# A linear-attention and SiLU feed-forward kernel: the tensor engine's tiles placed at multiples of 128 bytes

## The chip, the cores and the metric

The kernel runs on one core of one Trainium2 chip. The metric is the time of one execution in microseconds on the device, the median over several runs. TensorE does the matrix products; DVE (VectorE), ACT (ScalarE) and POOL (GpSimd) work on tiles elementwise; SP (SyncE) issues the DMAs. SBUF is the on-chip memory that holds 128 partitions; a tile occupies the same range of bytes in every partition. PSUM is the memory into which TensorE accumulates.

## The reference

```python
def _attn_ref(q, k, v, g_norm):          # q, k, v: 8 batches, 8 heads, 576 tokens, 64 wide
    kv = np.einsum('bhsd,bhse->bhde', k, v)
    out = np.einsum('bhsd,bhde->bhse', q, kv)
    rms = np.sqrt(np.mean(out * out, axis=-1, keepdims=True) + 1e-06)
    return (out / rms * g_norm).astype(np.float32)

def _moe_ref(x, w_in, w_out):            # x: 4608 x 512, w_in: 512 x 2048, w_out: 2048 x 512
    h = x @ w_in
    g = h * (1.0 / (1.0 + np.exp(-h)))
    return (g @ w_out).astype(np.float32)
```

The attention's output, heads side by side, is the `x` of the feed-forward part. All data is float32.

## The kernel before, in words

**Precision.** TensorE has a fast type for 4-byte operands, `float32r`, that keeps fewer bits than float32. The kernel splits an operand into an upper part in that type and the remainder, also in that type, and makes three products (upper by lower, lower by upper, upper by upper) that accumulate in one PSUM bank. A tile of such an operand therefore has a dimension of two, for the two parts. Products of plain float32 tiles are used where little is to be computed: k by v (L253), q by kv for the first two batches (L286, L341), transposes.

**Stages.** The 4608 tokens are nine tiles of 512. For each tile, the 16 blocks of `w_in` (128 features each) give h, transposed (features in the partitions, tokens along the row); ACT applies SiLU; the result is split into `gh` and `gl` and multiplied by the 16 blocks of `w_out` into four PSUM banks, one for each 128 tokens.

- Tiles 0 and 1 compute h plainly: `products` (L474) streams a slice of x (512 columns) against a 128x128 slice of the block `wi`, four slices by three products, twelve matmuls for a block. x of tile 0 lies in the tiles x0 to x3 (x0 to x2 in the `spare` places, x3 in a `late` place), x of tile 1 in `x_second`.
- Tiles 2 to 8 compute h in pairs of blocks by seven half-size products in place of eight, with sums of weights and sums of x: `pair_step` calls `product` (L634) seven times, each six matmuls of 256 columns, 42 for a pair and eight pairs for a tile. The streamed operands are made by `make_operand` in seven places: four in the memory of `x_second`, seen under another shape as `x_operands`, and three in the `spare` places (operand4 to operand6). The weights are slices of the `wi` blocks and of sums that are loaded back from DRAM.
- `project` (L505) multiplies `gh` and `gl` (as weights, 128x128) by `wo` (streamed, 512 columns): twelve matmuls for a block and tile. In the last tile, the last of the four banks is worked in two halves of 256 columns, the second of them in the bank `at`.
- Attention for later batches is fitted in between: k by v (L253), then q by kv in three products of 288 columns (L288 to L290) with the split tiles `kh` and `kl` as weights and `ql` and `qh` streamed.

**Order.** The order on each engine is written out by hand (`tc.manual_schedule()`): lists of jobs for each step, and a list `ORDER` for the loads on SP's queue. The products of `pair_step` and the projections alternate: 42 matmuls of L634, then 24 of L505, with the attention's products of four batches' pairs let in at two places in a tile.

**Places in SBUF.** Each pool hands out places in the order in which tiles or tags first appear, and a tile takes a multiple of 32 bytes in each partition. The pool `const` comes first: four `kvm` tiles (512 bytes each), `ident` (the tag `kh`, two places of 512), then `warm_up` and `gcol` (4 bytes, 32 taken), `both` (the tag `kl`, two places of 512), `d_eps` (32 taken), `x_place`, the three `spare` places, `gap`, the two `late` places. The pools of weights, k/v/q and gated tiles follow. `x_second` is the beginning of `x_place`, and `x_operands` is the same memory 48 elements (192 bytes) further on; the tile `gap` of 16 elements brings the two to 64 elements in all.

Of the kernel before, what the change touches and what calls it, by code (L numbers as in the profile page):

```python
# [8 lines left out]
F32 = mybir.dt.float32  # L9
F32R = mybir.dt.float32r  # L10
# [20 lines left out]
def linear_attention_rms_silu_ffn(  # L31
# [22 lines left out]
    nc = tc.nc  # L54
    B, NP, P, S = q.shape
# [3 lines left out]
    TN = 512  # L59
# [5 lines left out]
    const = ctx.enter_context(tc.tile_pool(name="const", bufs=1))  # L65
# [13 lines left out]
        nc.gpsimd.memset(t, 0.0)  # L79
    ident = const.tile([P, P], F32, name="ident", tag="kh", bufs=2)  # L80
    make_identity(nc, ident)
    warm_up = const.tile([P, 1], F32, name="warm_up")
    nc.gpsimd.memset(warm_up, 1.0)
    gcol = const.tile([P, 1], F32, name="gcol")
    both = const.tile([P, P], F32, name="both", tag="kl", bufs=2)
    nc.gpsimd.tensor_copy(out=both, in_=ident)
    for i in range(4):
        nc.gpsimd.tensor_copy(
            out=both[32 * i:32 * i + 32, 32 * (i ^ 1):32 * (i ^ 1) + 32], in_=ident[32 * i:32 * i + 32, 32 * i:32 * i + 32]
        )  # L90
    d_eps = const.tile([P, 1], F32, name="d_eps")
    nc.gpsimd.memset(d_eps, float(D) * EPS)

    def load_g():
        for h in range(P // D):
            nc.sync.dma_start(out=gcol[h * D:(h + 1) * D, :], in_=g_norm.rearrange("(d o) -> d o", o=1))
# [6 lines left out]

    SHIFT = 48
    x_place = const.tile([P, NP * 2 * TN + SHIFT], F32R, name="x_place")
    x_second = x_place[:, :NP * 2 * TN].rearrange("p (c a n) -> p c a n", c=NP, a=2)
    x_operands = x_place[:, SHIFT:].rearrange("p (c a k n) -> p c a k n", c=NP, a=2, k=2)  # L110
    x_first, lates = {}, {}

    def spare(n, shape, dtype, name):
        return const.tile(shape, dtype, name=name, tag=f"spare{n}")

    def late(n, shape, dtype, name):
        if not lates:
            const.tile([P, 64 - SHIFT], F32, name="gap")
        if name not in lates:
            lates[name] = const.tile(shape, dtype, name=name, tag=f"late{n}")  # L120
        return lates[name]

    def x32(c, w):

        return late(c // 2, [P, 2, TN], F32, f"x32_{c // 2}")[:, c % 2, w]
# [14 lines left out]
    def full_tile(kind, f):  # L140
        if kind == "wo":
            t = late(1, [P, 2, NP * P], F32, "wo_full")[:, f % 2]
        else:
            t = tmp.tile([P, S], F32, name="full", tag="tmp")[:, :NP * P]
        fulls[kind, f] = t
        return t
# [54 lines left out]
    def x_part(t, a, c):  # L201

        if t == 1:
            return x_second[:, c, a]
        if c not in x_first:
            kind = {"shape": [P, 2, TN], "dtype": F32R, "name": f"x{c}"}
            x_first[c] = spare(c, **kind) if c < 3 else late(0, **kind)
        return x_first[c][:, a]
# [386 lines left out]
    def operand(j):  # L595

        if j < 4:
            return x_operands[:, j]
        if j not in operands:
            operands[j] = spare(j - 4, [P, 2, 2, H], F32R, f"operand{j}")  # L600
        return operands[j]
# [20 lines left out]
    def make_operand(m):  # L622
        j, x, _ = seven[m]
        upper, lower = operand(j)[:, 0], operand(j)[:, 1]
        nc.scalar.copy(out=upper, in_=x())
        nc.vector.tensor_tensor(out=lower, in0=x(), in1=upper.bitcast(F32), op=ALU.subtract)

    def product(m, i, out):
        j, _, a_of = seven[m]
        x = operand(j)  # L630
        n = 0
        for c in range(2):
            for a, b in ((0, 1), (1, 0), (0, 0)):
                nc.tensor.matmul(  # L634
                    out=out, lhsT=a_of(i, a, c), rhs=x[:, b, c], start=(n == 0), stop=(n == 5)
                )
                n += 1
# [165 lines left out]
    with tc.manual_schedule():  # L803
# [4 lines left out]
        for item in ORDER.split():  # L808
            kind, n = item.rstrip("0123456789"), int(item.lstrip("wiopbg") or 0)
# [236 lines left out]
```

## Time and profile before

| | |
|---|---|
| median of 3 runs | 839.21 us (839.19 to 839.67) |
| profiled execution | 839.63 us, of which the span of the profile is 837.8 us |
| TensorE matmuls | 5454, busy 826.8 us, 99% of the span |
| TensorE weight loads | 5454, busy 734.6 us (88%), beside the matmuls |
| DVE, ACT, POOL | busy 63%, 43%, 17% |
| granted clock of TensorE | full throughout |
| DMA | 122.55 MB, on the mean 146 GB/s |

A matmul of the profile is two rows: PEld is its weight load, PE the streaming of the other operand through the array. Several are in flight, so the duration of one (389 ns for 512 columns on the page) is not the distance to the next one. That distance, the step, is read where a run of n matmuls stands as one piece: in the chain (each line: start in us, duration in us, what) or from starts in the timeline.

### The profile page before, as it was taken

To read this page: it belongs to the slowest core of one execution; us is meant where nothing else is said; L and a number is where in the kernel's file an instruction comes from. 1 tells how busy PE (TensorE), PEld (TensorE's weight loads), DVE (VectorE), ACT (ScalarE), POOL (GpSimd) and SP (SyncE) were. 2 spreads that over 40 slices of the span, in tenths; PEclk is the share of its full clock that TensorE was granted. 3 is DMA by queue.
4 is the path that set the end of the run, shared out by engine and by line. 5 is a ranking of instruction groups with operands and counts; after the bars stand their busy time and mean duration, and the time that the engine had idled before them with its cause. 6 is when DMAs were issued, how large, how long until landed. Compare 5 with 4: busy or idle time off the path is not lost.

```text
span 837.8 us, 14032 instructions
## 1 busy us (share of the span) xinstructions
PE 826.8 (99%) x5454; PEld 734.6 (88%) x5454; DVE 528.9 (63%) x1027; ACT 359.0 (43%) x744; POOL 145.9 (17%) x142
## 2 busy tenths in 40 slices
PE   8999999999999999999999999999999999999998
PEld 7767888888899999998999998999999999999997
DVE  4886875788476567657766667656865664464332
ACT  3766564534453245325532355225532432243222
POOL 2786983423010002000200011001100000000000
PEclk9999999999999999999999999999999999999999
DMA  8879011337343634364424452444423343334331
GB/s 322 313 257 362 4 57 51 136 145 261 122 161 100 215 115 146 101 214 144 165 91 160 163 173 88 158 158 157 151 84 103 106 155 103 105 102 151 100 102 51
DMA packets 42418, 122.55 MB, mean 146 GB/s; under 512 B 4848, under 2 KB 5104, under 8 KB 42352
## 3 DMA queue, kind: packets, MB, share of 16 engines
q1 hardware_dynamic: 42352, 121.65, 42.4%
q8 instruction: 43, 0.70, 0.4%
q14 instruction: 23, 0.19, 0.1%
HBM read 103.81 MB, written 17.83 MB: 145 GB/s over the span
## 4 chain that ended last, share of the span: by engine, by line
PE 94%; DMA 4%; POOL 1%; ACT 0%; issue 0%; SPq 0%
PE acc L505 46%; PE hp L634 33%; PE hp L474 9%; PE at L253 2%; DMA k<-in_k 1%; DMA wo<-in_moe_w_out 1%; DMA early_wi<-in_v 1%; DMA v<-in_v 1%; PE at L289 1%; PE at L288 1%; PE at L290 1%; PE at L505 1%; DMA wi<-in_moe_w_in 1%; PE at L286 1%; POOL wo L191 0%
## 5 line engine op out<-in xcount | busy, mean ns | idle before, releaser
L505 PE MATMUL acc<-wo,gh 128*128 128x512 f32 (+1 forms) x1152 | 354.1, 389 | 0.1
L505 PEld LDWEIGHTS acc<-wo,gh 128*128 128x128 f32 x1152 | 210.3, 188 | 39.7 <-POOL wo L191 0.3
L505 PE MATMUL acc<-wo,gl 128*128 128x512 f32 x576 | 223.0, 387 | 0.5 <-POOL gl L485 0.5
L634 PE MATMUL hp<-x_place,wi 128*128 128x256 f32 x1344 | 167.8, 280 | 0.0
L634 PEld LDWEIGHTS hp<-x_place,wi 128*128 128x128 f32 x1344 | 162.0, 189 | 0.0
L634 PEld LDWEIGHTS hp<-operand,wi 128*128 128x128 f32 x1008 | 126.0, 189 | 3.9
L505 PEld LDWEIGHTS acc<-wo,gl 128*128 128x128 f32 x576 | 108.1, 188 | 23.5 <-POOL gl L485 0.9
L634 PE MATMUL hp<-operand,wi 128*128 128x256 f32 x1008 | 127.5, 281 | 0.0
L275 POOL TENSOR_TENSOR ql<-q,qh 128x576 fp32r<-128x576 f32 x24 | 35.6, 1483 | 376.0 <-ACT qh L274 341.9
L685 ACT COPY wi<-hp 128x256 f32<-128x256 f32 x56 | 20.9, 373 | 140.9 <-PE hp L634 140.9
L643 ACT ACTIVATE gh<-gf 128x512 fp32r<-128x512 f32 x56 | 35.4, 633 | 94.4 <-DVE gf L698 81.6
L643 ACT ACTIVATE gh<-wi 128x512 fp32r<-128x512 f32 x56 | 35.5, 634 | 79.8 <-DVE wi L698 68.0
L686 DVE TENSOR_TENSOR gf<-hp,wi 128x256 f32<-128x256 f32 x28 | 11.9, 425 | 84.8 <-ACT wi L685 84.8
L686 DVE TENSOR_TENSOR wi<-hp,wi 128x256 f32<-128x256 f32 x28 | 11.9, 424 | 84.3 <-ACT wi L685 84.3
L474 PE MATMUL hp<-x,wi 128*128 128x512 f32 x180 | 46.4, 402 | 1.4 <-POOL wi L191 1.4
L474 PE MATMUL hp<-x_place,wi 128*128 128x512 f32 x192 | 46.4, 390 | 0.0
L647 DVE TENSOR_TENSOR gl<-wi,gh 128x512 fp32r<-128x512 f32 x56 | 38.4, 685 | 11.4 <-ACT wi L644 11.4
L687 DVE TENSOR_TENSOR wi<-hp,wi 128x256 f32<-128x256 f32 x56 | 23.8, 425 | 32.3 <-PE hp L634 32.3
L647 DVE TENSOR_TENSOR gl<-gf,gh 128x512 fp32r<-128x512 f32 x56 | 39.0, 696 | 7.3 <-ACT gf L644 7.3
L294 ACT ACTIVATE sq<-at 128x288 f32<-128x288 f32 x56 | 22.9, 410 | 45.6 <-PE at L290 38.9
L474 PEld LDWEIGHTS hp<-x_place,wi 128*128 128x128 f32 x192 | 35.7, 188 | 7.3
L316 DVE SCALAR_TENSOR_TENSOR x<-o,gcol,yT 128x128 f32<-128x128 f32 (+7 forms) x52 | 40.7, 784 | 1.9
(142 smaller groups left out, 1006.8 us busy)
## 6 DMA issues: line engine op xcount, KB each, us to landing
wi<-sums_in_dram SPq DMA_DIRECT2D x112, 512.0 KB, 3.3
out<-ob SPq DMA_DIRECT2D x35, 256.0 KB, 2.4
wi<-in_moe_w_in SPq DMA_DIRECT2D x16, 512.0 KB, 7.8
wo<-in_moe_w_out SPq DMA_DIRECT2D x16, 512.0 KB, 8.9
sums_in_dram<-sum_parts SPq DMA_DIRECT2D x16, 512.0 KB, 2.6
k<-in_k SPq DMA_DIRECT2D x28, 288.0 KB, 5.2
v<-in_v SPq DMA_DIRECT2D x28, 288.0 KB, 5.4
q<-in_q SPq DMA_DIRECT2D x28, 288.0 KB, 4.0
```

The lines of the kernel that those rows point to most:

```text
L253: nc.tensor.matmul(out=self.kv[h], lhsT=self.k[rows, c, :], rhs=self.v[rows, c, :], start=(start and r == 0), stop=(stop and r == 4),)
L275: nc.gpsimd.tensor_tensor(out=self.ql, in0=self.q, in1=self.qh.bitcast(F32), op=ALU.subtract)
L294: nc.scalar.activation(out=self.sq[:, self.w], in_=self.ps, func=AF.Square)
L316: nc.vector.scalar_tensor_tensor(out=to, in0=self.o[:, a:e], scalar=gcol, in1=self.yT, op0=ALU.mult, op1=ALU.mult)
L474: nc.tensor.matmul(out=hp[:, :TN], lhsT=w[:, a, fs], rhs=x_part(t, b, c), start=(c == 0 and i == 0), stop=(c == NP - 1 and i == 2),)
L505: nc.tensor.matmul(out=bank, lhsT=g[:, ns], rhs=w[:, a, cs], start=(f == first and i == 0), stop=(f == last and i == 2))
L634: nc.tensor.matmul(out=out, lhsT=a_of(i, a, c), rhs=x[:, b, c], start=(n == 0), stop=(n == 5))
L643: nc.scalar.activation(out=gh, in_=x, func=AF.Silu)
L647: nc.vector.tensor_tensor(out=gl, in0=x, in1=gh.bitcast(F32), op=ALU.subtract)
L685: nc.scalar.copy(out=p1, in_=u)
L686: nc.vector.tensor_tensor(out=c1[:, low], in0=v, in1=p1, op=ALU.add)
L687: nc.vector.tensor_tensor(out=u2, in0=y, in1=p1, op=ALU.add)
```

## The change

The small tiles `warm_up`, `gcol` and `d_eps` and a new tile `gap` of 8 elements now stand together behind `both`: four times 32 bytes. The shift of 48 elements, the tile `x_place` that made room for it and the old `gap` go. `x_second` is a tile of its own, and the four operands in its memory begin where it begins. By the order of allocation every tile that TensorE reads then begins at a multiple of 128 bytes in its partition. No computation changes, and no instruction is added or taken out.

```diff
-    warm_up = const.tile([P, 1], F32, name="warm_up")
-    nc.gpsimd.memset(warm_up, 1.0)
-    gcol = const.tile([P, 1], F32, name="gcol")
     both = const.tile([P, P], F32, name="both", tag="kl", bufs=2)
     nc.gpsimd.tensor_copy(out=both, in_=ident)
     for i in range(4):
...
+    warm_up = const.tile([P, 1], F32, name="warm_up")
+    nc.gpsimd.memset(warm_up, 1.0)
+    gcol = const.tile([P, 1], F32, name="gcol")
     d_eps = const.tile([P, 1], F32, name="d_eps")
     nc.gpsimd.memset(d_eps, float(D) * EPS)
+    const.tile([P, 8], F32, name="gap")
...
-    SHIFT = 48
-    x_place = const.tile([P, NP * 2 * TN + SHIFT], F32R, name="x_place")
-    x_second = x_place[:, :NP * 2 * TN].rearrange("p (c a n) -> p c a n", c=NP, a=2)
-    x_operands = x_place[:, SHIFT:].rearrange("p (c a k n) -> p c a k n", c=NP, a=2, k=2)
+    x_second = const.tile([P, NP, 2, TN], F32R, name="x_second")
...
     def late(n, shape, dtype, name):
-        if not lates:
-            const.tile([P, 64 - SHIFT], F32, name="gap")
         if name not in lates:
...
         if j < 4:
-            return x_operands[:, j]
+            return x_second[:, j].rearrange("p a (k n) -> p a k n", k=2)
```

## The prediction

> **What bounds the kernel now.** I read the page first (busy shares, clock, chain by line), then the chain in order of time stage by stage, then the timeline at the end of the last tile.
>
> ```profile
> span 837.8 us, 14032 instructions
> PE 826.8 (99%) x5454; PEld 734.6 (88%) x5454; DVE 528.9 (63%) x1027; ACT 359.0 (43%) x744; POOL 145.9 (17%) x142
> PEclk9999999999999999999999999999999999999999
> PE acc L505 46%; PE hp L634 33%; PE hp L474 9%; PE at L253 2%; DMA k<-in_k 1%; DMA wo<-in_moe_w_out 1%; DMA early_wi<-in_v 1%; DMA v<-in_v 1%; PE at L289 1%; PE at L288 1%; PE at L290 1%; PE at L505 1%; DMA wi<-in_moe_w_in 1%; PE at L286 1%; POOL wo L191 0%
> ```
>
> TensorE is busy for 99% of the span at full clock, and its matmuls are the chain. Its weight loads run beside the matmuls of the step before, 88% busy themselves. So what matters is the step from one matmul to the next, and nothing on another engine can hide a longer step. The busy table does not show it (pipelined matmuls overlap there); the chain does, since a piece of n matmuls lasts n steps.
>
> **Where the tiles lie.** Sum up the allocations in order, a small tile taking 32 bytes, from a pool that starts at a multiple of 128. Modulo 128, before: `kvm`, `kh` at 0, `kl` at 64; `x_second`, x3, all weight blocks, k/v/q and gh/gl at 96; `x_operands`, x0 to x2 and operand4 to 6 at 32. Slices inside tiles move by multiples of 128. After: everything at 0. Call the distance between the streamed operand and the weights that are loaded during it D. Before, D is 0 in L505 (wo against gh/gl, both 96) and in tile 1's L474 (x_second against wi), 64 in all of L634 and for x0 to x2 in tile 0's L474. After, D is 0 everywhere. The trace therefore already has both cases of D, though none with both streams at 0 in this matmul type.
>
> The chain, steps of 512 columns: tile 0 (nine of twelve L474 at D = 64, three at 0), then tile 1 (all at 0), with L505 beside them; and later tiles.
>
> ```profile
> 104.07 2.73 PE acc L505 x12
> 106.81 2.79 PE hp L474 x12
> 109.59 2.73 PE acc L505 x12
> 112.33 2.79 PE hp L474 x12
> ...
> 126.21 2.72 PE hp L474 x12
> 128.93 2.72 PE acc L505 x12
> 131.65 2.72 PE hp L474 x12
> ...
> 259.01 5.44 PE acc L505 x24
> 264.44 4.95 PE hp L634 x42
> ```
>
> At D = 0 a 512-column step is 2.72/12 = 0.2267 us (5.44/24 gives the same). In tile 0 it is 2.79/12 on the mean, so the nine at D = 64 take about (2.79 - 3 x 0.2267)/9 = 0.234. The address relation does set the step, by 3%.
>
> Steps of 256 columns, L634 at D = 64, in three settings, and L505's halves in the last tile at D = 0:
>
> ```profile
> 229.98 2.83 PE hp L634 x24
> 232.81 0.13 PE at L288
> ...
> 233.21 2.06 PE hp L634 x18
> ...
> 756.64 4.95 PE hp L634 x42
> ...
> 766.76 0.36 PE at L505 x3
> 767.12 4.78 PE hp L634 x42
> ```
>
> Entered from a 512-column run, L634 steps by 4.95/42 = 0.1179 (2.83/24 likewise). Entered from the 288-column products or from 256-column ones it steps by 2.06/18 = 0.1144 and 4.78/42 = 0.1138. So D = 64 has two steady steps, chosen by the entry. At D = 0 the halves step by 0.36/3 = 0.120. The timeline of the last halves gives the same from starts three apart:
>
> ```profile
> 833.26 0.28 PE L505 MATMUL acc<-wo,gl 128*128 128x256 f32 x1
> 833.26 0.31 PEld L505 LDWEIGHTS acc<-wo,gh 128*128 128x128 f32 x2
> ...
> 833.62 0.28 PE L505 MATMUL acc<-wo,gl 128*128 128x256 f32 x1
> ...
> 833.98 0.28 PE L505 MATMUL at<-wo,gl 128*128 128x256 f32 x1
> ...
> 834.34 0.28 PE L505 MATMUL at<-wo,gl 128*128 128x256 f32 x1
> ```
>
> 1.08 us over nine steps is 0.120 again, whichever PSUM bank is written.
>
> **What a step holds over its columns.** The plain-float products of L286 (same 288 columns, two passes) show a rate with room to spare:
>
> ```profile
> 58.06 0.48 PE at L286 x2
> ```
>
> 0.24 per pass against 0.13 at L288: if a pass takes two clocks a column, a clock is 0.24/576 = 0.417 ns, and 512 and 256 columns need 0.2133 and 0.1067. At D = 0 the excess is 0.2267 - 0.2133 = 0.0133 and 0.120 - 0.1067 = 0.0133: the same for both lengths. An excess that goes by the matmul and not by its columns is what one weight load beside it would cost if the two reads get in each other's way; at D = 64 it is 0.021 for 512 columns, 0.011 or 0.007 for 256. I take it that distance matters and the common start does not: at 0/0 the excess is that of 96/96.
>
> The Trainium skill, TensorE: Matmul & The Clock Gate, Part 2 (step 1), says the opposite: two independent SBUF read ports, so loading the next weights takes no read bandwidth from the running matmul. By it D would change no step, and the sum would be nothing. The trace differs: 2.79 against 2.72 us for twelve equal products. The same skill's SBUF — State Buffer (Specifications) gives lines of 16 bytes; by that, starts at 32 and 96 were line starts already, and the move to 0 gains nothing by itself. No run here shows that yet.
>
> **The change part by part.** No instruction is added or removed; operands move.
>
> 1. L634, 2352 products, D from 64 to 0. No row has 256 columns of this line at D = 0; the nearest is L505's halves at 0.120. Bounds: 0.1138 (the quick step of the row above) below, 0.120 above; a bound still lower is the second rival. I take 0.120, because it is the steady step at the D that comes. The page shows 56 groups (8 per tile, 7 tiles). 40 of 42 at 4.95 go to 5.04: 40 x 0.09 = +3.6. Ten are split into 24 at 2.83 (to 2.88, +0.5) and 18 at 2.06 (to 2.16, +1.0). The last tile's six of 42 at 4.78 (to 5.04) give +1.6. Sum +6.7. If those entered after 288 or 256 columns keep their quick step it is +4.1.
> 2. Tile 0's x0 to x2, D from 64 to 0: 2.79 to 2.72 in some 13 pieces on the chain, -0.9. Where a POOL or ACT wait ends last (below), the gain goes to that wait; it is at most 13 x 0.07.
>
> ```profile
> 61.81 0.41 ACT sq L294
> 62.22 0.30 ACT o L295
> 62.52 0.04 issue
> 62.56 0.95 PE at L253 x20
> 63.51 2.99 PE hp L474 x12
> ```
>
> 3. L288 to L290 (144 products, 288 columns): D from 96 (kh) and 32 (kl) to 0. Now 0.13 each; 288 x 0.417 ns + 0.0133 = 0.133 against about 0.131: +0.3. Bounds: 144 x (0.120 - 0.131) = -1.6 and 144 x 0.010 = +1.4.
> 4. L505's 1680 whole products and tile 1's L474 keep D = 0: nothing. Their common start moves from 96 to 0, which no row prices; the ends are the second and fourth rivals.
> 5. The gap tile is written and read by nobody, and SP's queue keeps its order. `warm_up`'s and `d_eps`'s memsets may come after the copies into `both` on POOL, about 1.2 us later (0.29 + 0.94). The queue behind them on POOL is empty until the first splits, and ACT does not need `warm_up` before its table load is over nor `d_eps` before 10.73:
>
> ```profile
> 1.44 0.10 POOL L83 MEMSET warm_up<- 128x1 f32 x1
> 1.96 0.29 POOL L86 COPY both<-ident 128x128 f32<-128x128 f32 x1
> 2.31 0.94 POOL L88 COPY both<-ident 32x32 f32<-32x32 f32 x4
> 0.73 1.28 ACT L828 ACT_TABLE_LOAD   x1 [0.73 <-PEq L1032]
> 7.63 0.43 ACT L261 COPY kvm<-hp 64x64 f32<-64x64 f32 x2 [5.40 <-PE hp L253]
> 10.73 0.27 ACT L403 ACTIVATE y<-at,d_eps 128x8 f32<-128x8 f32 x1 [0.83 <-DVE at L402]
> ```
>
> ACT idles 5.40 before its next work, which covers it; without that cover it would cost 1.2 us.
>
> Sum: +6.7 - 0.9 + 0.3 = +6.1. The profiled execution took 839.63 (span 837.8 and 1.83 around it), so 845.7, and a span of 843.9. The median of the runs is 0.42 lower, 839.21; on it the forecast is 845.3.
>
> **The rivals.**
> - The quick step takes over: at 0/0 L634 settles at 0.1138 whatever came before. 40 x (4.78 - 4.95) - 10 x (2.83 - 2.73) - 0.9 = -8.7: 830.5. For it: the quick step exists in the same addresses (4.78). Against: at D = 0 the halves do not keep it, at 0.36 per three. Chance 0.20.
> - The common start matters: with both streams on a 128-byte boundary the excess goes away. 512 columns at 0.2133: 1872 x -0.0133 = -25, tile 0 -3, L634 at 0.1138 -8: some 803 (786 if 256 columns came down to 0.1067 too). Against: L288 to L290 load weights at 0 and 64 and are still 0.010 over their columns. Chance 0.10.
> - Nothing changes that can be measured (0.2%, about 1.7 us, is what a measurement of this kernel tells from no change): steps hang on entry alone, and D is a coincidence of stages. Against: 2.79 and 2.72 alternate with the same neighbours. 839 to 840, chance 0.12.
> - 512 columns at 0/0 fall into tile 0's slow step: 1872 x 0.0067 = +12.5 on top, 858. Only the start could do that. Chance 0.08.
> - The loads get quicker and steps stay. The chain before 37.6 us is DMA (below). A 4096-byte row that starts at 96 modulo 128 touches one 256-byte piece more than the sixteen it needs; 1/17 of 35 us is at most -2: 837. Nothing on the page shows such a cost. Chance 0.05. The Trainium skill, DMA: Bandwidth & Descriptors (How a descriptor splits into AXI transactions), has transfers begin at 256-byte boundaries, which is such a rule; no run here shows it.
>
> ```profile
> 7.04 7.28 DMA early_wi<-in_v
> 14.33 8.24 DMA wo<-in_moe_w_out
> 22.59 8.41 DMA k<-in_k
> 31.01 6.57 DMA v<-in_v
> ```
>
> **How the numbers follow.** The forecast's case has 0.45, its own range 843 to 848 (from the +4.1 of step 1 to the upper bound of step 3). Slower 0.45 + 0.08 = 0.53, within 0.2% 0.12, faster 0.20 + 0.10 + 0.05 = 0.35. A range from 828 to 850 leaves out the second and fourth rivals, 0.18.
>
> **What would show it.** Right: L634 pieces of 42 at 5.04 in every tile, the last one too; tile 0's L474 at 2.72; L505 still 5.44 per 24; L288 to L290 at 0.13. Wrong: L505 pieces away from 5.44 (the start matters, either way), or L634 at 4.78 or 4.95. An earlier end of the first DMA pieces would speak for the last rival.

## The result, and the profile after

The changed kernel takes 845.73 us, the median of four runs (845.24 to 845.97), against 839.2 of the kernel before: 1.0076 times as long, 95% interval 1.0058 to 1.0093. The profiled execution took 845.76 us, with a span of 843.9. The forecast was 845.3 and a span of 843.9.

First the page of the changed kernel: its head, the chain by line, and the groups of those of the seven products that stream from the memory of `x_second`. Its lines are three lower than before: L631 is the old L634 (seven products), L471 the old L474 (tiles 0 and 1), L502 the old L505 (projection), L285 to L287 the old L288 to L290.

```profile
span 843.9 us, 14033 instructions
PE 833.1 (99%) x5454; PEld 741.1 (88%) x5454; DVE 529.0 (63%) x1027; ACT 359.3 (43%) x744; POOL 146.0 (17%) x142
...
PEclk9999999999999999999999999999999999999999
...
PE acc L502 46%; PE hp L631 33%; PE hp L471 9%; PE at L250 2%; DMA wo<-in_moe_w_out 1%; DMA k<-in_k 1%; DMA v<-in_v 1%; PE at L286 1%; PE at L285 1%; PE at L287 1%; DMA wi<-in_moe_w_in 1%; DMA early_wi<-in_v 1%; PE at L502 1%; PE at L283 1%; POOL wo L188 0%
...
L631 PE MATMUL hp<-x_second,wi 128*128 128x256 f32 x1344 | 172.0, 283 | 0.0
L631 PEld LDWEIGHTS hp<-x_second,wi 128*128 128x128 f32 x1344 | 166.1, 192 | 0.0
```

The same two groups on the page of before:

```profile
L634 PE MATMUL hp<-x_place,wi 128*128 128x256 f32 x1344 | 167.8, 280 | 0.0
L634 PEld LDWEIGHTS hp<-x_place,wi 128*128 128x128 f32 x1344 | 162.0, 189 | 0.0
```

The same 5454 matmuls, full clock, TensorE 99% busy, the other engines' busy time the same within 0.3 us: only TensorE's steps got longer. The weight load beside them is longer too, 192 ns where the page of before had 189.

Then the chain of the changed kernel in order of time (start, duration in us, what): tile 0, tile 1, the first pair of tile 2 and what follows, and the last tile from its second pair on.

```profile
100.40 2.72 PE hp L471 x12
103.12 2.72 PE acc L502 x12
...
130.47 2.72 PE hp L471 x12
...
221.21 5.03 PE hp L631 x42
226.24 2.75 PE acc L502 x12
228.99 2.87 PE hp L631 x24
...
231.99 0.14 PE at L286
...
232.26 2.16 PE hp L631 x18
...
258.37 5.47 PE acc L502 x24
263.84 5.03 PE hp L631 x42
...
761.00 5.03 PE hp L631 x42
766.04 2.42 PE acc L502 x12
768.46 0.36 PE at L502 x3
...
771.60 5.04 PE hp L631 x42
```

Where the time went is read from the starts of equal pieces. Those of before are in the prediction, but for the first pair of tile 2:

```profile
222.31 4.95 PE hp L634 x42
```

Tile 1's piece that began at 131.65 before begins at 130.47: 1.18 us were gained by then. The first pair begins at 221.21 in place of 222.31. The second pair of the last tile begins at 761.00 in place of 756.64, its third pair at 771.60 in place of 767.12: +4.4 and +4.5. The rest is lost from there to the end, in the last six pairs, whose products took 4.78 before and now take 5.04.

### The profile page after: what moved, and what is told of

Read it like the earlier page. It is cut to its first block, busy times and chain, and to the rows that moved or that the text cites. A ratio compares the mean times of both kernels' runs of the same rounds, so it can differ in the third digit from the quotient of the medians.

```text
span 843.9 us, 14033 instructions
## 1 busy us (share of the span) xinstructions
PE 833.1 (99%) x5454; PEld 741.1 (88%) x5454; DVE 529.0 (63%) x1027; ACT 359.3 (43%) x744; POOL 146.0 (17%) x142
## 4 chain that ended last, share of the span: by engine, by line
PE 94%; DMA 4%; POOL 1%; ACT 0%; issue 0%; SPq 0%
PE acc L502 46%; PE hp L631 33%; PE hp L471 9%; PE at L250 2%; DMA wo<-in_moe_w_out 1%; DMA k<-in_k 1%; DMA v<-in_v 1%; PE at L286 1%; PE at L285 1%; PE at L287 1%; DMA wi<-in_moe_w_in 1%; DMA early_wi<-in_v 1%; PE at L502 1%; PE at L283 1%; POOL wo L188 0%
## 5 line engine op out<-in xcount | busy, mean ns | idle before, releaser
L502 PE MATMUL acc<-wo,gh 128*128 128x512 f32 (+1 forms) x1152 | 354.8, 389 | 0.1
L502 PEld LDWEIGHTS acc<-wo,gh 128*128 128x128 f32 x1152 | 210.6, 188 | 40.0 <-POOL wo L188 0.3
L502 PE MATMUL acc<-wo,gl 128*128 128x512 f32 x576 | 223.0, 387 | 0.5 <-POOL gl L482 0.5
L631 PE MATMUL hp<-x_second,wi 128*128 128x256 f32 x1344 | 172.0, 283 | 0.0
L631 PEld LDWEIGHTS hp<-x_second,wi 128*128 128x128 f32 x1344 | 166.1, 192 | 0.0
L631 PEld LDWEIGHTS hp<-operand,wi 128*128 128x128 f32 x1008 | 128.0, 191 | 4.0
L631 PE MATMUL hp<-operand,wi 128*128 128x256 f32 x1008 | 129.7, 283 | 0.0
L502 PEld LDWEIGHTS acc<-wo,gl 128*128 128x128 f32 x576 | 108.2, 188 | 23.7 <-POOL gl L482 0.9
L471 PE MATMUL hp<-x,wi 128*128 128x512 f32 x180 | 45.7, 399 | 1.5 <-POOL wi L188 1.5
L471 PE MATMUL hp<-x_second,wi 128*128 128x512 f32 x192 | 46.4, 390 | 0.0
L471 PEld LDWEIGHTS hp<-x_second,wi 128*128 128x128 f32 x192 | 35.7, 188 | 7.3
```

The source lines that it names most:

```text
L471: nc.tensor.matmul(out=hp[:, :TN], lhsT=w[:, a, fs], rhs=x_part(t, b, c), start=(c == 0 and i == 0), stop=(c == NP - 1 and i == 2),)
L502: nc.tensor.matmul(out=bank, lhsT=g[:, ns], rhs=w[:, a, cs], start=(f == first and i == 0), stop=(f == last and i == 2))
L631: nc.tensor.matmul(out=out, lhsT=a_of(i, a, c), rhs=x[:, b, c], start=(n == 0), stop=(n == 5))
```

## The experiments

Every kernel is compared with the kernel before on the same chip. D is the distance of the prediction: place of the streamed operand less place of the weights. "Seven products" means the line that is L634 in the kernel before.

**1. Is it the common start, or the distance?** The kernel before with no shift has D = 0 again, with streams and weight blocks at 96 modulo 128 in place of 0.

```diff
-    SHIFT = 48
+    SHIFT = 0
```

> The kernel before with a shift of 0: every stream and every weight block at 96 modulo 128, so the distance D between streamed operand and weights is 0 as in the changed kernel, but the common start is 96 in place of 0. Distance theory (only D modulo 128 counts): 42 products of L634 in 5.03 us in every tile, 12 of tile 0 in 2.72, total 845.7, the same as the changed kernel within 0.2%. Rival, common start (a multiple of 128 is what costs): L634 at 4.95 and the total near 839.

Measured 845.01 us, 1.0071 (1.0054 to 1.0087). The chain of this run:

```profile
252.97 5.03 PE hp L634 x42
258.01 5.47 PE acc L505 x24
...
770.86 5.04 PE hp L634 x42
```

Within 0.01 us a piece, these are the pieces of the changed kernel, at another start. That the tiles begin at multiples of 128 costs nothing and brings nothing; that the shift is gone costs the time.

**2. The distance alone, in seven values.** The changed kernel, with the streamed operands N elements of four bytes further on and weights and everything behind them left at 0 modulo 256 (x0 to x2 share the moved places).

```diff
-    x_second = const.tile([P, NP, 2, TN], F32R, name="x_second")
+    SHIFT = N
+    x_place = const.tile([P, NP * 2 * TN + SHIFT], F32R, name="x_place")
+    x_second = x_place[:, :NP * 2 * TN].rearrange("p (c a n) -> p c a n", c=NP, a=2)
+    x_operands = x_place[:, SHIFT:].rearrange("p (c a k n) -> p c a k n", c=NP, a=2, k=2)
...
+        if not lates:
+            const.tile([P, 64 - SHIFT], F32, name="gap2")
...
-            return x_second[:, j].rearrange("p a (k n) -> p a k n", k=2)
+            return x_operands[:, j]
```

N = 16, 64 bytes:

> The changed kernel with the streamed operands of L634 (and x0 to x2) 64 bytes further on, weights left at 0 modulo 128: D = 64 as before, at other places than before (64 and 0 in place of 32 and 96). Distance theory: L634 again 4.95 per 42 after a 512-column run, 2.06 per 18, 4.78 in the last tile; tile 0's twelve back to 2.79; total 839.3. Rival, place of the stream alone (32 modulo 128 was the good place): no return, 845 to 846.

N = 8, 32 bytes:

> The changed kernel with the streamed operands of L634 and x0 to x2 32 bytes further on: D = 32. No row has 256 columns at this D. Distance theory with the excess of the 288-column products of before (D = 96 and 32, 0.010 over their columns): 42 in 4.91, total about 839; tile 0's twelve in 2.69. Rival, only two classes (same place or not): exactly the times of D = 64, 4.95 and 2.79, total 839.3.

N = 24, 96 bytes:

> The changed kernel with the streamed operands of L634 and x0 to x2 96 bytes further on: D = 96. Distance theory: as for D = 32 by the 288-column rows, 42 in 4.91, about 839; if the sign of D matters (the stream runs ahead of the weights or behind), this run differs from D = 32. Rival, two classes: 4.95 and 2.79, 839.3.

64 bytes gave 841.78 us (1.0030, 1.0019 to 1.0042), 32 gave 839.28 (1.0001, 0.9991 to 1.0010), 96 gave 847.71 (1.0102, 1.0087 to 1.0117). So a move of 32 bytes brings the lost time back, and one of 96 loses more. Only the forecast for 32 came near, and only for the products of 256 columns: 42 take 4.90 (forecast 4.91), while tile 0's twelve take 2.79 (forecast 2.69). The forecasts of 839.3 for 64 and of 839 for 96 were missed. The chains of 32 and of 96, tile 0 and then a pair:

```profile
89.02 2.79 PE hp L476 x12
...
263.60 4.90 PE hp L636 x42
```

```profile
83.91 2.81 PE hp L476 x12
...
264.69 5.04 PE hp L636 x42
```

For 256 columns, neither the place of the stream (32 good) nor two classes (same place or not) explains three different values. But 64 bytes did not bring back the kernel before: its chain has 4.95 everywhere, the last tile too, and 2.12 per 18.

```profile
331.20 2.83 PE hp L636 x24
...
334.44 2.12 PE hp L636 x18
...
343.28 4.95 PE hp L636 x42
...
768.35 4.95 PE hp L636 x42
```

In the kernel before the operands lie at 160 and the weights at 224 modulo 256, which is 192 and not 64. So N = 48, 192 bytes:

> The changed kernel with the streamed operands of L634 and x0 to x2 192 bytes further on, weights at 0: D is 64 modulo 128 as in the run with 64 bytes, but 192 modulo 256, as in the kernel before (160 against 224). The run with 64 bytes stepped by 0.1178 everywhere and never showed the quick step of before (4.78 per 42, 2.06 per 18). If the distance counts modulo 256: the quick step is back, and the total is that of before, 839.2. If modulo 128: as with 64 bytes, 841.8, and the quick step belongs to the common start.

Measured 839.02 us (0.9999, 0.9989 to 1.0009), and the chain is that of the kernel before, with the weights at 0:

```profile
241.41 2.83 PE hp L636 x24
...
244.63 2.06 PE hp L636 x18
...
253.43 4.95 PE hp L636 x42
...
766.34 4.78 PE hp L636 x42
```

So a distance of 64 and one of 192 are not the same: the distance does not count modulo 128. That a further 256 bytes change nothing is seen in the first experiment. There the tile `gap` takes 256 bytes between streams and weights, so the distance is 256 and not 0 when it is counted modulo 512, and the pieces are those of the changed kernel, which has no such tile. As far as this one pair shows, it counts modulo 256. The other three values:

> The changed kernel with the streamed operands of L634 and x0 to x2 128 bytes further on: still multiples of 128, D = 128. If the distance counts modulo 128, the times are those of the changed kernel: 0.120 a step, 42 in 5.04, 845.5. If it counts modulo 256 (as 64 and 192 differ: 841.8 and 839.0), this is a place of its own; by the mean of its neighbours 96 and 160 nothing firm can be said, 838 to 848.

> The same with 160 bytes, D = 160. Modulo 128 this is 32 and would repeat that run: 0.1167 everywhere, the last tile 0.1178, 839.3. Modulo 256 the neighbour 192 has the two steps 0.1178 and 0.1138, so the quick one may be reached here too: 838 to 840.

> The same with 224 bytes, D = 224. Modulo 128 this is 96 and would repeat that run: 0.1202, 847.7. Modulo 256 it is a place of its own next to 192 and 0: between 839 and 845.7.

They gave 846.8 us (1.0091, 1.0076 to 1.0106), 842.42 (1.0039, 1.0025 to 1.0053) and 841.9 (1.0032, 1.0019 to 1.0046). The forecast for 160 (838 to 840) was missed: its pairs do not reach the quick step. A pair each of 160 and of 224, from their chains:

```profile
263.86 4.99 PE hp L636 x42
```

```profile
263.88 4.97 PE hp L636 x42
```

32 and 160 differ (4.90 and 4.99), and so do 96 and 224 (5.04 and 4.97). Of distances 128 apart, 0 and 128 have nearly the same pieces of 42, and 64 and 192 have them after 512 columns alone. All eight distances, from the chains:

| D, bytes modulo 256 | 42 products after 512 columns | 18 after 288 columns | 42 after halves of 256 columns (last tile) | tile 0's twelve of 512 columns | ratio to the kernel before |
|---|---|---|---|---|---|
| 0 (the changed kernel) | 5.03 | 2.16 | 5.04 | 2.72 | 1.0076 |
| 32 | 4.90 | 2.10 | 4.95 | 2.79 | 1.0001 |
| 64 | 4.95 | 2.12 | 4.95 | 2.78 | 1.0030 |
| 96 | 5.04 | 2.16 | 5.04 | 2.81 | 1.0102 |
| 128 | 5.04 | 2.16 | 4.99 | 2.79 | 1.0091 |
| 160 | 4.99 | 2.12 | 4.93 | 2.79 | 1.0039 |
| 192 (as before) | 4.95 | 2.06 | 4.78 | 2.79 | 0.9999 |
| 224 | 4.97 | 2.12 | 4.97 | 2.79 | 1.0032 |

Tile 0's twelve (nine of them at D, three at 0; the commonest piece is given) behave otherwise than the products of 256 columns. There the two classes do fit: 2.72 at the same place, 2.78 to 2.81 at each of the seven others.

**3. The distance in the projection.** In the kernel before, `gh` and `gl`, the weights of the projection, are moved by a tile ahead of them in their pool: 24 elements put them at 64 modulo 256 (D = 224 - 64 = 160, which is 32 modulo 128), 16 put them at 32 (D = 192, which is 64 modulo 128). All else lies as before.

```diff
+    gp.tile([P, 24], F32, name="gap_gp", bufs=1)
     kvm = [const.tile([P, P], F32, name=f"kvm{i}") for i in range(NP)]
```

> The kernel before with gh and gl (the weights of L505) 96 bytes further on: D of L505 goes from 0 to 32 (wo at 96, gh at 64 modulo 128), all else as before. Distance theory, with L634's 0.1168 at D = 32 (excess 0.010) carried over to 512 columns: 24 of L505 in 5.36, 1728 steps less 3 ns, 834. With tile 0's rows at D = 32 (its twelve no quicker than at D = 64): 0.233, 24 in 5.6, 850. Rival, distance matters only where weight load and stream take the same time (256 columns): 5.44, 839.

> The kernel before with gh and gl 64 bytes further on: D of L505 from 0 to 64 modulo 128, all else as before. Distance theory by tile 0's L474 at D = 64: 0.2333 a step, 24 in 5.60, 1728 x 0.0066 = +11, 850.5. Rival, distance matters only for 256 columns and tile 0's 2.79 belonged to its stage: 5.44, 839.

Measured 843.21 us (1.0049, 1.0033 to 1.0065) and 845.91 (1.0082, 1.0066 to 1.0098). The chain of the first, then of the second:

```profile
260.79 5.61 PE acc L506 x24
266.40 4.79 PE hp L635 x42
```

```profile
260.58 5.60 PE acc L506 x24
266.18 4.78 PE hp L635 x42
...
345.50 4.95 PE hp L635 x42
...
356.05 4.78 PE hp L635 x42
```

Here 512 columns step by 0.233 in place of 0.2267, as tile 0's nine slow products did: 5.60 was forecast to the digit. The saving that I had held possible at D = 32 is refuted, by 5.61 at 160 and by tile 0's 2.79 at 32. Both totals forecast by tile 0's rows (850 and 850.5) were too high. By the starts, the projection takes 9.4 us longer in the first run and 8.1 in the second, and not 11: its runs of nine between the attention's products stay at 2.10 (2.08 and 2.09 before). The rest of the gap is L634, which takes 5.3 and 1.5 us less. At unchanged places it now takes its quick step, 4.78 in place of 4.95, in 34 (first run) and 19 (second) of the 40 groups that were slow before. What ran before it had changed, its own addresses had not. In the second run the six groups of the last tile, which were quick before, are slow, although halves of 256 columns run ahead of them as they did:

```profile
771.73 0.34 PE at L506 x3
772.07 4.95 PE hp L635 x42
```

The halves lie at D = 192 there. The entry is therefore not set by the length of what runs before alone; its distance has a part. The distance that is best for 256 columns is not best for 512, and the entry is a second cause of its own.

**4. The entry.** In the kernel before, the last projection ahead of the 42 products is worked in two halves, so that six matmuls of 256 columns come before them (except at the end of a tile):

```diff
+        if groups and groups[-1][1] != order(groups[-1][0])[-1] and groups[-1][-1] == slice(0, DM):
+            *head, bank, n, _ = groups.pop()
+            groups += [(*head, bank[:, s], n, s) for s in (slice(0, DM // 2), slice(DM // 2, DM))]
```

> The kernel before, where the last projection ahead of a pair's 42 products is worked in two halves of 256 columns (same columns, same sums, six matmuls for three), as the last tile does anyway. Entry theory (which of two steady steps L634 takes at D = 64 is set by what ran just before): 42 in 4.78 for most of the 40 that took 4.95, -0.17 each, less 0.04 for the six matmuls: about 834.5. Rival, the quick step belongs to the last tile (less work on other engines, no DMA of sums): 4.95 stays, +0.04 each, 841.

Measured 834.29 us, 0.9941 (0.9926 to 0.9957). Its chain:

```profile
253.04 4.78 PE hp L634 x42
257.82 5.49 PE acc L505 x27
263.30 4.78 PE hp L634 x42
```

42 products go from 4.95 to 4.78, and the projection from 5.44 to 5.49, as forecast. The last tile's quick step in the kernel before is therefore not a matter of that tile's lighter load on other engines. By the chain, 37 of the 40 groups of 42 that took 4.95 before are now quick.

The last run asks how little is enough: only the last of the three matmuls is halved. It also moves x1 and x2 of tile 0 to D = 0, within the same memory. The core of the edit:

```diff
-            nc.tensor.matmul(
-                out=bank, lhsT=g[:, ns], rhs=w[:, a, cs], start=(f == first and i == 0), stop=(f == last and i == 2)
-            )
+            for s in (slice(0, DM // 2), slice(DM // 2, DM)) if halves and i == 2 else (cs,):
+                nc.tensor.matmul(
+                    out=bank[:, s] if halves else bank, lhsT=g[:, ns], rhs=w[:, a, s],
+                    start=(f == first and i == 0), stop=(f == last and i == 2),
+                )
...
-            x_first[c] = spare(c, **kind) if c < 3 else late(0, **kind)
+            x_first[c] = spare(c, **kind, more=64 - SHIFT if c else 0) if c < 3 else late(0, **kind)
```

> The kernel before with only the last matmul ahead of a pair's 42 products worked in two halves of 256 columns (one more matmul in place of three more), and x1 and x2 of tile 0 placed 64 bytes further on, at D = 0 against the weights, while the operands of L634 in the same memory stay where they were. Entry theory, if two halves are enough: 42 in 4.78 as with six, -0.17 x 35, +0.013 for each extra matmul: -5.4; tile 0's twelve in 2.74 by the distance theory (six of nine slow ones put right), -0.6; total about 833.2. If the entry needs a longer run of 256-column steps: 4.95 stays and the total is 839.2, less the 0.6 of tile 0.

Measured 832.58 us, 0.9922 (0.9909 to 0.9936): quicker than both kernels, and the best of the study. Its chain, tile 0 and then the pairs of tile 2:

```profile
105.80 2.76 PE hp L479 x12
...
257.65 5.46 PE acc L511 x25
263.11 4.78 PE hp L641 x42
```

Two steps of 256 columns, with the projection at D = 0, are enough for the quick step (4.78), and the extra matmul costs 0.02 (5.44 to 5.46). Tile 0's twelve are at 2.76, about half way from 2.79 to 2.72, where six of nine moved products were expected to give 2.74.

## Why the prediction was right, and where it was not

- **The mechanism, that the distance between streamed operand and weights sets the step and their common start does not.** Right, and shown: start 96 and start 0 give the same pieces at D = 0 (5.03 and 5.04), and the 192-byte run, at another start than the kernel before, has its pieces at its distance (4.95, 2.06, 4.78). That the two reads get in each other's way in SBUF is only argued: no run took the weight load away. It is also open whether the weights that count are those loaded during a product or its own, since in every long run both have the same distance.
- **"Modulo 128".** Wrong as a rule, with no harm to the number, because the change went to 0 from 192 and 0 is slow under both. With the rule as the prediction had it, 64 bytes would have been as good as before; it cost 0.3%.
- **Step 1, L634 +6.7.** Nearly exact. 4.95 became 5.03, 2.83 became 2.87, 2.06 became 2.16, 4.78 became 5.04. By the starts of its matmuls (the time from the start before to each start, added up by line) this line takes 6.3 us longer. The choice of 0.120 over the quick 0.1138, also for the groups entered from shorter products, was the one that mattered: in the changed kernel no entry leads to a quick step.
- **Step 2, tile 0 -0.9.** The mechanism is right (2.79 to 2.72), the size somewhat too large. By 130.47 the profile is 1.18 ahead, but 0.46 of it was there at the first product of L286 (below), which is scatter of the loads; 0.7 is left, and by the starts of its matmuls the line of tiles 0 and 1 takes 0.6 less.
- **Step 3, L288 to L290 +0.3.** Too high: the pieces stay at 0.13 and 0.14, and by their starts the three lines together differ by less than 0.1 us. The row that was carried over (one excess for all lengths at D = 0) was not theirs: `kh` and `kl` lie ahead of the four small places of 32 bytes and q behind them, so in the changed kernel these products are at D = 128 modulo 256, not at 0.
- **Step 4, L505 0.** Mis-sized: the run of 24 takes 5.47 and not 5.44. By the starts, the first five steps after the products of D = 0 take 0.233, 0.236, 0.228, 0.233 and 0.231, and only then 0.2267; the line takes 0.85 longer in all. This is an entry cost again, in the other direction.
- **The sum, +6.1.** It was exact by luck: the products gave 6.3 and not 6.7, tile 0 -0.6 and not -0.9, L288 to L290 nothing and not 0.3, the projection 0.85 and not nothing, and the scatter of the loads -0.46, which no term held. These errors cancel.
- **Step 5, the memsets: nothing.** Right; TensorE's first pieces stand where they stood.
- **The other rivals.** The quick step does not take over at D = 0: after 288 columns 18 products take 2.16, in the last tile 42 take 5.04. A boundary of 128 bytes takes no excess away (L502 at 5.47, the same 5.47 at start 96), and 512 columns do not fall into tile 0's slow step (2.72).
- **The fifth rival, quicker loads.** The first product of L286 in the changed kernel, and in the halved-projection run, which has the places of the kernel before:

```profile
46.97 0.75 PE at L283 x2
```

```profile
46.48 0.75 PE at L286 x2
```

In the kernel before:

```profile
47.43 0.75 PE at L286 x2
```

The run with unchanged places is earlier still, so 0.46 lies within the scatter between executions, and no effect of 256-byte starts can be told from it. The rule of the Trainium skill that was named beside this rival, DMA: Bandwidth & Descriptors (How a descriptor splits into AXI transactions), is not visible in this kernel's time.
- **The rule of two independent read ports**, in the Trainium skill's TensorE: Matmul & The Clock Gate, Part 2 (step 1), by which nothing should have moved: the trace does not agree. Equal products after the same run of 512 columns step by 0.117 to 0.120 by distance alone (4.90 to 5.04 per 42).

## What to carry to other kernels

Where TensorE is the bound and a weight load runs beside every matmul, look at the steps (duration of a long run in the chain over its count), stage by stage, and at the places of the two operands relative to each other, not at round addresses. Here distance was worth 1% and what runs just before a stage another 0.6%. A folk rule such as "align everything" makes all distances equal, which is one particular distance: here a slow one for products of 256 columns (5.03 per 42) and the quick one for 512 (2.72 per 12).

## What the runs showed of the hardware that was not expected

- The distance counts modulo 256 bytes and not 128: 42 products of 256 columns take 4.90 at 32 and 4.99 at 160, 5.04 at 96 and 4.97 at 224.
- The step has memory. At a distance of 192 the same 42 products at the same places run at 4.95 or 4.78, for the whole run, by what ran in the two steps before, their distance included; at the seven other distances the pieces changed by at most 0.06 with the entry (4.99 and 4.93 at 160).
- 512 and 256 columns want different distances: at 192 the one loses (5.44 to 5.60 per 24) where the other gains (5.03 to 4.95 or 4.78 per 42). For 512 columns only D = 0 is quick (2.72 per twelve), and the seven other distances cost nearly the same (2.78 to 2.81); for 256 columns there are at least five different steps.
